# Conversion units among the experts on ScalarE's DMA queue, begun one unit ahead; x rows stored later; the last hidden tile halved first

## The chip, the cores and the metric

The kernel runs on one core of a Trainium2 chip. The metric is device time in microseconds of one execution. The engines are TensorE (PE), VectorE (DVE), ScalarE (ACT), GpSimd (POOL) and SyncE (SP); each works through its own instructions in order and waits for the others on semaphores. SyncE computes nothing and issues DMAs; ScalarE and GpSimd can issue DMAs too, from a queue of their own.

## The reference

Three stages follow one another.

- Attention for 4 batches and 12 heads, 448 positions, head size 64: `sigmoid(q k^T / 8 - log 448) v`. The heads are put side by side: x, 1792 rows of 768.
- A mixture of 8 experts: each row is routed to the expert with the largest cosine logit; `gate * (relu(x @ w1[e]) @ w2[e])`, with 1024 hidden columns.
- An FFN over all rows: `h = x @ w_in`, ELU, `@ w_out`, with 2048 hidden columns. `w_in` and `w_out` arrive as 64-bit floats.

## The kernel before

**Halves.** A float32 operand of a matmul is split into a high part (a ScalarE copy to a rounded type) and a low part (source minus high part, on VectorE), and each product is three matmuls: high by high, high by low, low by high. In `parts` these are lines 347 and 348; in `halves` lines 411 and 414.

**Attention.** Work goes by head pairs p = 0 to 23, six pairs to a batch. A pair has four quarters; in them TensorE does the scores of pair p (`S_part`, line 947), the products with v of pair p - 1 (`A_part`, line 966), and the transposes of q and k for pair p + 2 (`T_part`), which ScalarE and VectorE evacuate (lines 936, 938, 940). A list `late` holds jobs of the batch just finished, one taken in a quarter: logits, and `xrows`, which transposes x back to rows in a tile X (evacuated by VectorE, line 1051). `xstore` writes X to DRAM (line 1061). For the third batch the list also holds `early_a`, `early_b` and `early_c`; these find the rows of the first expert window from the first three batches and gather them (line 1139) for `x_first` (line 688), and from `early_b` on the first expert's weights are loaded.

**Conversion.** `conv_steps` turns the 64-bit words of `w_in` (layer 0, during the attention) and `w_out` (layer 1, among the experts) into float32 blocks, with sums of blocks for a seven-product (Strassen) FFN, and stores 28 blocks a layer to DRAM (`wdram`). It is a generator; `conv()` advances it by one step at places written out by hand. A layer has 16 units of 768 KB. A unit u has

- a load into tile c64 (tag c64, three buffers), issued by SyncE;
- a head: VectorE takes the upper word's magnitude bits into tile cm (line 146, which waits for the load), and GpSimd clamps it (line 150, "the clamp");
- step A (lines 200 to 220): VectorE puts sign, exponent and mantissa together (lines 209, 213), and the load of unit u + 2 is issued;
- step B (lines 221 to 237): VectorE adds the low word's share (lines 221, 224; the last reader of c64), and GpSimd adds the two parts into the result (line 234, "the add");
- step C (lines 238 to 242): the head of unit u + 2, then VectorE's sums for the unit before (line 169). Stores are issued four flushes after they are noted.

In the attention `conv()` stands in three of four quarters, from pair 2 on; among the experts it stands four times in a window.

**Experts.** Rows are sorted by expert into windows of 128; there are 19 in the regular loop here. Window w does the first layer of window w + 1 in four tiles (`L1_tile`, lines 707 to 709) with a conversion step after each, after the second of them the transposes of its own hidden rows (`hT_part`: line 728, hh on ScalarE at line 738, hl on VectorE at line 740), then the transposes of gathered rows for w + 2 (line 670, xh at 674, xl at 675), then its second layer in four tiles (`L2_tile`, line 769), and the gated evacuation y (line 751). The hidden rows come from ScalarE at line 713. Where a window has a new expert, weights are halved inside `tc.If`, and SyncE reloads the freed buffer with a conditional DMA:

```python
def parts_if(w, slots):
    with tc.If(new_of(w)):
        for slot in slots:
            parts(slot, nc.vector)
    for slot in slots:
        ...
        load_w(int(slot < 4), slot % 4, e, new=reg(nc.sync, "new", w))
```

`window(w)` calls it after its second and fourth second-layer tile, for w + 1 (second-layer weights) and w + 2 (first-layer weights). These loads are in the program whether or not the condition holds, each with its waits. At window 14 the conversion's memory is handed over to a tile r1, into which ScalarE's queue loads rows of y (line 423); from window 14 on rows of y are transposed and summed for the FFN.

**FFN.** `f1` (lines 1488 to 1490) and `f2` (lines 1620 to 1622) take 112 converted blocks, loaded by SyncE (line 385) and halved by `split_to`. B11, T2 and B21 are operands of x for it, the first units of which are halved around the last window.

Of the kernel before, what the change touches and what calls it, by code (L numbers as in the profile page):

```python
# [26 lines left out]
def kernel(  # L27
# [80 lines left out]
    w_out_b = w_out.bitcast(U32)  # L108
    NQ = F2 // 2 // 256

    def conv_steps(layer, cv, j0=0, j1=NQ):
        raw, mags, hf, sums, out = {}, {}, {}, [], []
        now = [0]

# [3 lines left out]
        def load(u):  # L118
            if u >= n:
                return  # L120
            j, qi = divmod(u, 4)
            r, c = quarters[qi]
            t = cv.tile([P, CU, 2], U32, tag="c64", bufs=3, name=f"c64_{layer}_{u}")
            raw[u] = t
            if layer == 0:
                c0 = 2 * (c * F2 // 2 + 256 * j)
                nc.sync.dma_start(
                    out=t.rearrange("p (k f) t -> p k (f t)", k=3),
                    in_=w_in_b[384 * r:384 * (r + 1), c0:c0 + 512].rearrange(
                        "(k p) f -> p k f", p=P  # L130
                    ),
                )
            else:
                r0 = r * F2 // 2 + 256 * j
                nc.sync.dma_start(
                    out=t.rearrange("p (k f) t -> p k (f t)", k=2),
                    in_=w_out_b[r0:r0 + 256, DM * c:DM * (c + 1)].rearrange(
                        "(k p) f -> p k f", p=P
                    ),
                )  # L140

        def head(u):
            if u >= n:
                return
            mags[u] = cv.tile([P, CU], U32, tag="cm", bufs=3, name=f"cm_{layer}_{u}")
            nc.vector.tensor_scalar(  # L146
                out=mags[u], in0=raw[u][:, :, 1], scalar1=0x7FFFFFFF, scalar2=None,
                op0=ALU.bitwise_and,
            )
            nc.gpsimd.tensor_scalar(  # L150
                out=mags[u].bitcast(F32), in0=mags[u].bitcast(F32), scalar1=F64_LEAST,
                scalar2=F64_MOST, op0=ALU.max, op1=ALU.min,
            )
# [5 lines left out]
        def flush(every=False):  # L159
            now[0] += 1  # L160
            while out and (every or out[0][0] <= now[0]):
                _, i, t = out.pop(0)
                nc.sync.dma_start(out=wdram[i], in_=t)

        def stile(name):
            return cv.tile([P, CU], F32, tag="cs", bufs=4, name=name)
# [28 lines left out]
            load(4 * j0 + u)  # L195
        yield
        head(4 * j0)
        head(4 * j0 + 1)
        yield
        for u in range(4 * j0, n):  # L200
            j, qi = divmod(u, 4)
# [16 lines left out]
            if u > 4 * j0:  # L218
                load(u + 2)
            yield  # L220
            nc.vector.tensor_scalar(
                out=mag, in0=cat, scalar1=0xFF800000, scalar2=None, op0=ALU.bitwise_and
            )
# [11 lines left out]
            sums.append((j, qi))  # L235
            flush()
            yield
            head(u + 2)
            if len(sums) > 1:
                group(*sums.pop(0))  # L240
            flush()
# [168 lines left out]
    def half_hi(src, hi):  # L410
        nc.scalar.activation(out=hi, in_=src, func=AF.Copy)  # L411
# [31 lines left out]
    def x_split(g, name):  # L443
        halves(xf[g][name], *xs2[g][name])
# [355 lines left out]
        for n in ("T1", "T2", "T3", "T4"):  # L800
            x_sum(0, n, slice(i * P, (i + 1) * P))

    def window(w, first, end, mid=None, turn=None):
        if w + 1 < end:
            more = w + 1
        else:
            more = None
        for t in range(4):
            if more:
                L1_tile(more, t)  # L810
            if t == 0:
                if w + 3 < end:
                    gather(w + 3)
                if w > max(first, 1):
                    scatter(w - 1)
            if t == 1:
                if w == 1:
                    route_step()
                hT_part(w, 1 if more else 2)
                if w == 1:  # L820
                    y_out(0)
                    scatter(0)
            conv(1)
        if w + 2 < end:
            xT_part(w + 2)
        if turn:
            turn()
        for t in range(4):
            L2_tile(w, t)
            if mid and t in mid:  # L830
                mid[t]()
            if t % 2 and first == 0:
                if w + 1 < end:
                    parts_if(w + 1, (3 + t, 4 + t))
                if w + 2 < end:
                    parts_if(w + 2, (t - 1, t))
# [28 lines left out]
    with ExitStack() as actx:  # L865
# [39 lines left out]
        nc.sync.dma_start(out=embt, in_=emb)  # L905
        nc.sync.dma_start(out=rtau, in_=tau.partition_broadcast(P))
        load(1, "qkv")
        conv_it[0] = conv_steps(0, cva)
        conv()

        pairs = [(b, hp) for b in range(B) for hp in range(NPAIR)]
# [236 lines left out]
        def after_pair(p):  # L1148
# [3 lines left out]
            if hp == NPAIR - 1:  # L1152
# [6 lines left out]
                late.append(lambda: xrows(b, 2, 1))  # L1159
                if b == B - 2:  # L1160
                    late.append(early_a)
                late.append(lambda: (xrows(b, 3, 1), xstore(b)))
                if b == B - 2:
                    late.append(early_b)
                if b == B - 2:
                    late.extend([lambda: None] * 2 + [early_c])
                squares.extend((b, c) for c in range(NCH))

        pw = ps_s.tile([P, 2, 512], F32, tag="s", name="pw")[:, 0, :]
# [104 lines left out]
    with mctx:  # L1274
# [50 lines left out]
        for w in range(1, NA):  # L1325
            if w == 4:
                n_win = nc.values_load(nwi, min_val=0, max_val=NW)
            if w == 2:
# [2 lines left out]
                cvb = yctx.enter_context(  # L1331
                    tc.tile_pool(name="cvb", bufs=1, side="right", reuse_waits="tile")
                )
                conv_it[0] = conv_steps(1, cvb)
                conv(2)
            if w == CE:
                def x_early(g):
# [27 lines left out]
                for u in range(4):  # L1365
                    load_u(u)
            else:
                window(w, 0, NA, turn=lambda: (x_split(0, "B11"), split_to(0)),
                       mid={1: lambda: (x_split(0, "T2"), split_to(1))})
                half_hi(xf[0]["B21"], xs2[0]["B21"][0])  # L1370
                split_to(2)
        scatter(NA - 1)
        with tc.If(n_win > NA):
            for w in range(NA, NW):
# [318 lines left out]
```

## Time and profile before

| | |
|---|---|
| runs | 1119.63 us median of 3 (1117.32 to 1122.5) |
| profiled execution | 1115.99 us, span 1114.1 us |
| TensorE busy | 1015.3 us (91% of the span) |
| VectorE busy | 747.9 us (67%) |
| ScalarE busy | 549.6 us (49%) |
| GpSimd busy | 269.0 us (24%) |
| mean granted TensorE clock | 0.966 of full speed |
| DMA | q1 (SyncE) 151.83 MB, q10 (ScalarE) 4.72 MB, q0 (GpSimd) 18.49 MB |

The attention takes about the first 230 us, the experts up to 655 us, the FFN the rest. Times in the views count from the start of the span. A row of a timeline gives start, duration, engine, line, operation and tiles, and in brackets how long the engine had been idle and what ended that. A row of the windows view gives a stretch, its length, the busy time and instruction count of PE, PEld (weight loads), DVE, ACT and POOL, the granted TensorE clock (1.00 is 2.4 GHz, the lower level 1.2 GHz is 0.5), and the DMA engines' busy share and rate in GB/s.

### The profile page before, as it was taken

The numbers are of one execution on the slowest core, as the hardware profiler recorded it, in microseconds if no ns is written. First come the engines' busy times: TensorE is split into PE (matmuls) and PEld (weight loads), VectorE is DVE, ScalarE is ACT, GpSimd is POOL, SyncE is SP. The second block draws the span as 40 slices with busy tenths as digits, with TensorE's granted clock in tenths as the row PEclk, the third lists the DMA queues.
The fourth block names the chain that finished last, engine by engine and source line by source line (L and its number), as shares of the span: only waits on it lengthen the run. The fifth ranks groups of instructions, "written<-read, shape, count | busy, mean of one in ns | idle before, by whom it ended". The sixth has DMA issues, their size and how long they took to land. (4 is left out here: it accounts for less than half of the span.)

```text
span 1114.1 us, 14875 instructions
## 1 busy us (share of the span) xinstructions
PE 1015.3 (91%) x5351; PEld 821.4 (74%) x5351; DVE 747.9 (67%) x853; ACT 549.6 (49%) x651; POOL 269.0 (24%) x189
## 2 busy tenths in 40 slices
PE   9997989988898797998989979999899999998997
PEld 5442434457797686987978967888898998997986
DVE  3898965376266484467335558888878578889883
ACT  6665566762224241234144556666643527677441
POOL 1665750054265253545201000000000040000002
PEclk9998999989999898999999989999899999999999
DMA  9678864544246676457266332332224353433342
GB/s 250 186 234 266 248 209 137 194 163 171 99 120 225 221 252 207 134 173 267 100 224 230 130 106 82 100 100 86 71 85 141 115 196 116 116 126 99 114 125 102
DMA packets 65520, 176.05 MB, mean 158 GB/s; under 512 B 6167, under 2 KB 22295, under 8 KB 64992
## 3 DMA queue, kind: packets, MB, share of 16 engines
q1 hardware_dynamic: 59840, 151.83, 43.1%
q0 software_dynamic: 4160, 18.49, 4.8%
q10 hardware_dynamic: 1440, 4.72, 1.2%
q8 instruction: 43, 0.70, 0.3%
q14 instruction: 37, 0.30, 0.1%
HBM read 211.98 MB, written 40.51 MB: 227 GB/s over the span
## 5 line engine op out<-in xcount | busy, mean ns | idle before, releaser
L150 POOL TENSOR_SCALAR cm<-cm 128x768 f32<-128x768 f32 x32 | 102.2, 3195 | 81.0 <-DVE cm L146 76.2
L708 PE MATMUL ph<-wl,xh 128*128 128x512 f32 x228 | 94.5, 415 | 20.9 <-DVEq L358 17.5
L769 PE MATMUL py<-wh,hh 128*128 128x384 f32 x304 | 106.1, 349 | 3.6 <-ACT hh L738 3.5
L348 DVE TENSOR_TENSOR wl<-raw,wh 128x1536 fp32r<-128x1536 f32 x44 | 76.3, 1775 | 43.5 <-ACT wh L347 42.9
L952 ACT ACTIVATE a<-ps,bias_s 112x896 f32<-112x896 f32 x96 | 91.6, 1002 | 26.2 <-PE ps L947 25.5
L769 PE MATMUL py<-wl,hh 128*128 128x384 f32 x304 | 103.6, 341 | 0.0
L707 PE MATMUL ph<-wh,xh 128*128 128x512 f32 x228 | 95.0, 417 | 7.1 <-ACT wh L347 5.5
L769 PE MATMUL py<-wh,hl 128*128 128x384 f32 x304 | 93.6, 339 | 0.1
L709 PE MATMUL ph<-wh,xl 128*128 128x512 f32 x228 | 93.0, 408 | 0.3 <-DVE xl L675 0.3
L947 PE MATMUL ps<-qk 64*112 64x448 f32 x384 | 87.7, 577 | 0.5 <-ACT a L952 0.5
L347 ACT ACTIVATE wh<-raw 128x1536 fp32r<-128x1536 f32 x48 | 69.2, 1481 | 31.5 <-DMA raw<-in_moe_w_dram 26.6
L414 DVE TENSOR_TENSOR wh<-raw,wh 128x768 fp32r<-128x768 f32 x65 | 61.8, 952 | 33.8 <-ACT wh L411 27.9
L966 PE MATMUL pav<-a,v 112*64 112x448 f32 x384 | 82.8, 553 | 0.0
L411 ACT ACTIVATE wh<-raw 128x768 fp32r<-128x768 f32 x65 | 54.4, 840 | 48.4 <-PE o L1622 31.4
L1621 PE MATMUL o<-wh,xr 128*128 128x384 f32 x196 | 68.7, 351 | 9.6 <-DVE wh L414 9.5
L708 PEld LDWEIGHTS ph<-wl,xh 128*128 128x128 f32 x228 | 45.4, 199 | 33.1 <-DVEq L358 19.3
L1620 PE MATMUL o<-wh,xr 128*128 128x384 f32 x196 | 67.3, 344 | 2.6 <-ACT wh L411 1.4
L1622 PE MATMUL o<-wh,xr 128*128 128x384 f32 x196 | 67.2, 343 | 2.3 <-DVE xr L414 2.3
L414 DVE TENSOR_TENSOR xr<-r,xr 128x1536 fp32r<-128x1536 f32 (+2 forms) x33 | 62.0, 1878 | 6.4 <-ACT xr L411 6.4
L740 DVE TENSOR_TENSOR hl<-pht,hh 128x1024 fp32r<-128x1024 f32 (+1 forms) x21 | 23.3, 1119 | 60.1 <-ACT hh L738 60.1
L966 PEld LDWEIGHTS pav<-a,v 112*64 112x64 f32 x384 | 23.5, 137 | 54.5 <-issue 51.6
L769 PEld LDWEIGHTS py<-wh,hh 128*128 128x128 f32 x304 | 58.5, 192 | 4.1 <-ACT hh L738 3.7
(291 smaller groups left out, 2500.9 us busy)
## 6 DMA issues: line engine op xcount, KB each, us to landing
raw<-in_moe_w_dram SPq DMA_DIRECT2D x142, 768.0 KB
raw<-wdram SPq DMA_DIRECT2D x112, 384.0 KB
c<-in_moe_w_in_dram SPq DMA_DIRECT2D x16, 768.0 KB
wdram<-ch SPq DMA_DIRECT2D x32, 384.0 KB
c<-in_moe_w_out_dram SPq DMA_DIRECT2D x16, 768.0 KB
wdram<-cs SPq DMA_DIRECT2D x24, 384.0 KB
v<-in_v_dram SPq DMA_DIRECT2D x12, 448.0 KB
xdram<-X SPq DMA_DIRECT2D x4, 1344.0 KB
```

Source lines behind the costliest of these rows:

```text
L150: nc.gpsimd.tensor_scalar(out=mags[u].bitcast(F32), in0=mags[u].bitcast(F32), scalar1=F64_LEAST, scalar2=F64_MOST, op0=ALU.max, op1=ALU.min,)
L347: nc.scalar.activation(out=wh, in_=raws[slot % 4], func=AF.Copy)
L348: eng.tensor_tensor(out=wl_, in0=raws[slot % 4], in1=wh.bitcast(F32), op=ALU.subtract)
L414: nc.vector.tensor_tensor(out=lo, in0=src, in1=hi.bitcast(F32), op=ALU.subtract)
L707: nc.tensor.matmul(o, lhsT=xh[:, kc, :], rhs=wh[:, sl], start=first, stop=False)
L708: nc.tensor.matmul(o, lhsT=xh[:, kc, :], rhs=wl_[:, sl], start=False, stop=False)
L709: nc.tensor.matmul(o, lhsT=xl[:, kc, :], rhs=wh[:, sl], start=False, stop=last)
L769: nc.tensor.matmul(py[:, n, :384], lhsT=a[:, f, :], rhs=b[:, i * 768 + n * 384:i * 768 + (n + 1) * 384], start=(f == 0 and a is hh and b i ...
L947: nc.tensor.matmul(ps[:CP, a, :S], lhsT=qk_t[p][r, 2, i * CP:(i + 1) * CP], rhs=qk_t[p][r, j, :], start=True, stop=True,)
L952: nc.scalar.activation(out=at, in_=ps[:CP, :, :S], func=AF.Sigmoid, bias=bias_s[:CP], scale=1.0 / math.sqrt(D),)
L966: nc.tensor.matmul(pav[p][j * D:(j + 1) * D, :S], lhsT=loaded[g][2][:, hh, c * D:(c + 1) * D], rhs=at_t[p, 2 * j + c // 2][:, c % 2, :], s ...
L1621: nc.tensor.matmul(o, lhsT=ah[:, c, ts_], rhs=wl_[:, sl], start=False, stop=False)
```

## The change

1. `conv_steps` takes the engine that issues its DMAs. Layer 0 stays on SyncE; all 16 loads and 28 stores of layer 1 go to ScalarE's queue.
2. The head of unit u + 1 is issued at the start of step B of unit u; before, the head of unit u + 2 was issued in step C of unit u. One unit's head, not two, is issued before the first step A. The tag cm has two buffers, not three.
3. `xstore` of the first two batches is taken from the list three jobs after the last `xrows` job; that of the third batch after `early_b`, two jobs after it. `early_c` keeps its place.
4. The last window's `hT_part` moves from that window into the one before it, behind its last second-layer tile and ahead of its `parts_if`. The halvings of B11 and unit 0 stand before the last window's first instruction, those of T2 and unit 1 after its first second-layer tile (before: after the second), those of B21 and unit 2 after its third (before: behind the window).

```diff
-    def conv_steps(layer, cv, j0=0, j1=NQ):
+    def conv_steps(layer, cv, eng, j0=0, j1=NQ):
...
-                nc.sync.dma_start(
+                eng.dma_start(
                     out=t.rearrange("p (k f) t -> p k (f t)", k=2),
...
-            mags[u] = cv.tile([P, CU], U32, tag="cm", bufs=3, name=f"cm_{layer}_{u}")
+            mags[u] = cv.tile([P, CU], U32, tag="cm", bufs=2, name=f"cm_{layer}_{u}")
...
                 _, i, t = out.pop(0)
-                nc.sync.dma_start(out=wdram[i], in_=t)
+                eng.dma_start(out=wdram[i], in_=t)
...
         head(4 * j0)
-        head(4 * j0 + 1)
         yield
...
             if u > 4 * j0:
                 load(u + 2)
             yield
+            head(u + 1)
             nc.vector.tensor_scalar(
                 out=mag, in0=cat, scalar1=0xFF800000, scalar2=None, op0=ALU.bitwise_and
             )
...
             flush()
             yield
-            head(u + 2)
             if len(sums) > 1:
                 group(*sums.pop(0))
...
-    def window(w, first, end, mid=None, turn=None):
+    def window(w, first, end, mid=None):
...
-                hT_part(w, 1 if more else 2)
+                if more:
+                    hT_part(w)
...
-        if turn:
-            turn()
         for t in range(4):
             L2_tile(w, t)
             if mid and t in mid:
                 mid[t]()
+            if t == 3 and w + 2 == end:
+                hT_part(w + 1, 2)
             if t % 2 and first == 0:
...
-        conv_it[0] = conv_steps(0, cva)
+        conv_it[0] = conv_steps(0, cva, nc.sync)
...
-                late.append(lambda: (xrows(b, 3, 1), xstore(b)))
+                late.append(lambda: xrows(b, 3, 1))
                 if b == B - 2:
                     late.append(early_b)
-                if b == B - 2:
-                    late.extend([lambda: None] * 2 + [early_c])
+                    late.extend([lambda: xstore(b), lambda: None, early_c])
+                else:
+                    late.extend([lambda: None] * 2 + [lambda: xstore(b)])
...
-                conv_it[0] = conv_steps(1, cvb)
+                conv_it[0] = conv_steps(1, cvb, nc.scalar)
...
-                window(w, 0, NA, turn=lambda: (x_split(0, "B11"), split_to(0)),
-                       mid={1: lambda: (x_split(0, "T2"), split_to(1))})
-                half_hi(xf[0]["B21"], xs2[0]["B21"][0])
-                split_to(2)
+                x_split(0, "B11")
+                split_to(0)
+                window(w, 0, NA, mid={
+                    0: lambda: (x_split(0, "T2"), split_to(1)),
+                    2: lambda: (half_hi(xf[0]["B21"], xs2[0]["B21"][0]), split_to(2)),
+                })
```

## Rows read from the trace of the kernel before

**Rows 1.** The waits, all engines: who waited for whom, us, times, longest
```profile
DVE cm L146 <- DMA c<-in_moe_w_out_dram: 41.8, 6, 13.3
...
DVE cm L146 <- DMA c<-in_moe_w_in_dram: 11.5, 2, 7.7
```

**Rows 2.** Windows: head pairs 4, 6, 10, 16; busy us, clock, DMA
```profile
39.20:47.93 8.73, 8.73 (x51) 4.00 (x49) 6.43 (x11) 5.43 (x7) 4.59 (x2) 1.00 0.66 191
56.03:63.79 7.76, 7.76 (x41) 3.03 (x40) 7.59 (x9) 5.43 (x8) 5.17 (x2) 1.00 0.86 243
90.30:108.50 18.20, 11.15 (x50) 4.78 (x49) 14.00 (x19) 7.34 (x12) 8.51 (x4) 0.81 0.98 287
151.50:167.33 15.83, 10.46 (x51) 4.69 (x49) 9.93 (x15) 7.35 (x12) 5.80 (x2) 0.89 0.74 231
```

**Rows 3.** Windows: expert windows 2, 5, 6, 8, 9, 12, 14, 15
```profile
292.80:317.92 25.12, 20.20 (x99) 18.36 (x99) 13.15 (x13) 3.83 (x5) 13.87 (x8) 0.86 0.48 159
354.13:380.52 26.39, 21.11 (x99) 18.33 (x98) 13.78 (x13) 6.46 (x7) 9.89 (x5) 0.87 0.60 197
380.52:408.28 27.76, 21.25 (x99) 18.46 (x99) 23.05 (x19) 12.31 (x11) 16.08 (x9) 0.82 0.75 252
427.48:453.66 26.18, 19.83 (x100) 17.55 (x100) 15.42 (x16) 3.72 (x5) 12.44 (x8) 0.87 0.56 185
453.66:471.76 18.10, 18.10 (x100) 16.55 (x100) 7.43 (x9) 3.73 (x5) 9.10 (x6) 1.00 0.41 134
510.68:534.96 24.28, 19.97 (x100) 17.63 (x100) 16.50 (x16) 6.46 (x7) 13.05 (x9) 0.93 0.59 200
553.06:579.36 26.30, 20.99 (x112) 19.08 (x112) 5.71 (x5) 8.34 (x11) 2.51 (x5) 0.94 0.48 169
579.36:599.70 20.34, 19.94 (x111) 17.75 (x111) 11.57 (x12) 11.08 (x13) 1.52 (x4) 1.00 0.68 227
```

**Rows 4.** Timeline of SyncE in window 5
```profile
358.15 16.11 SPq L338 DMA_DIRECT2D raw<-in_moe_w_dram  x8
...
374.32 0.40 SPq L135 DMA_DIRECT2D c<-in_moe_w_out_dram  x1
```

**Rows 5.** The waits of SyncE's own queue
```profile
SPq L1061 <- DVE X L1051: 38.9, 3, 21.8
```

**Rows 6.** Timeline of VectorE, pairs 4 and 5 and window 5
```profile
45.87 0.56 DVE L209 TENSOR_SCALAR cm<-cm 128x768 uint32<-128x768 uint32 x1
...
50.16 1.86 DVE L146 TENSOR_SCALAR cm<-c 128x768 uint32<-128x768 uint32 x1
...
379.91 0.56 DVE L146 TENSOR_SCALAR cm<-c 128x768 uint32<-128x768 uint32 x1 [8.55 <-DMA c<-in_moe_w_out_dram]
```

**Rows 7.** Timeline of GpSimd, the same pairs, and the first gather
```profile
44.34 2.77 POOL L150 TENSOR_SCALAR cm<-cm 128x768 f32<-128x768 f32 x1 [1.01 <-DVE cm L146]
...
49.79 1.81 POOL L234 TENSOR_TENSOR ch<-cm,cc 128x768 f32<-128x768 f32 x1 [2.67 <-DVE cm L224]
...
212.70 1.25 POOL L1139 DMA_INDIRECT xg<-xdram,idx  x1 [16.71 <-DMA xdram<-X]
```

**Rows 8.** Timeline of ScalarE at the start of window 14
```profile
563.37 1.81 ACTq L423 DMA_DIRECT2D r<-ydram  x4
...
565.28 1.02 ACT L738 ACTIVATE hh<-pht 128x1024 fp32r<-128x1024 f32 x1 [10.98 <-issue]
```

**Rows 9.** Timeline of TensorE: first gathered rows, last window, first FFN matmul
```profile
225.12 0.88 PE L688 MATMUL pxt<-ident,xg 128*128 128x128 f32 x6
...
644.57 0.45 PE L769 MATMUL py<-wh,hh 128*128 128x384 f32 x1 [3.48 <-ACT hh L738]
...
659.39 0.77 PE L1488 MATMUL f<-wl,wh 128*128 128x512 f32 x1 [4.37 <-DVEq L1373]
```

**Rows 10.** The page: a group of instructions, and a DMA's us to landing
```profile
L347 ACT ACTIVATE wh<-raw 128x1536 fp32r<-128x1536 f32 x48 | 69.2, 1481 | 31.5 <-DMA raw<-in_moe_w_dram 26.6
...
xg<-xdram,idx POOLq DMA_INDIRECT x1, 7.2
```

More of the change, by code (lines that the diff above doesn't have):

```diff
@@ L134, in load @@
                 r0 = r * F2 // 2 + 256 * j
-                nc.sync.dma_start(
+                eng.dma_start(
                     out=t.rearrange("p (k f) t -> p k (f t)", k=2),
```

## Prediction

> **What bounds the kernel now.** I began with the idle time of TensorE, because it is the engine that is busy nearly everywhere, and asked of each long gap what ended it. The waits give the first lead: VectorE waited 41.8 us in six places for the raw second-layer words (tile c, line 146, the head of a conversion unit) and 11.5 us in two places for the first-layer words [rows 1]. VectorE works in order, so whatever stands behind that head is late too: the evacuations of the attention's transposes, and in the experts the low halves of weights and the skipped `If` blocks that TensorE must see passed.
>
> Next I cut the span at stage borders. Head pairs 4, 10 and 16 do the same work in three batches (51, 50 and 51 recorded matmuls), but take 8.73, 18.20 and 15.83 us [rows 2]: the eight lost microseconds of each late pair are where the two waits of 11.5 us fall. An expert window without a wait takes 18.10 us (window 9), one with the extra rows of y 20.34 (window 15) [rows 3]. Against these, windows 2, 5, 6, 8, 12 and 14 are longer by 7.02, 8.29, 9.66, 8.08, 6.18 and 5.96 us. Not all of that is idle time. In window 8 TensorE idled 26.18 - 19.83 = 6.35 us, and its busy time is still 1.73 us above window 9's: after the idle stretch the granted clock averages 0.87, part of the window at the 1.2 GHz level and the rest at 2.4. So a long gap costs itself and some 1.7 us.
>
> Then SyncE, which issues all of these loads. In window 5 it spends 16.11 us on eight conditional weight loads, and only behind the last does the conversion's load leave, at 374.32; it lands at 379.9, where VectorE has idled 8.55 us [rows 4, 6]. The load was late in the queue, not long under way (5.6 us). In the attention the store of x rows holds the same queue for VectorE's last copy, 38.9 us in three waits [rows 5]. Last, two single gaps at the end of the experts: 3.48 us for hh of the last window, 4.37 us before the first FFN matmul [rows 9].
>
> **The change part by part.**
>
> *Experts: queue and order.* A load is issued at step A of the unit two before its own. Its head stood at step C of that same unit, two steps on; it moves to step B of the next, four steps on, which is one full window (18.10 us). Windows 5, 6, 8 and 12 wait because A and C fall into one window. On ScalarE's queue nothing conditional is ahead, so I expect all four waits to go. What comes instead: between a unit's head and its step A now lie the clamp (2.77 us) and, issued behind the clamp rather than before it, the add of the unit before (1.81 us) [rows 7]. That is 4.6 us on GpSimd, formerly spread over four steps. At best VectorE's own work covers it, at worst none; I take 2.3 us for windows 5, 6 and 12, where weights are halved right behind, and nothing for window 8, which has slack. Saved: 8.29 - 2.3 = 6.0, 9.66 - 2.3 = 7.4, 6.18 - 2.3 = 3.9 and 8.1 us, in all 25.4 (bounds 12.7, if contention with the weights keeps half, and 32.2).
>
> *Window 2.* Its first loads stay just ahead of their use, and they follow the evacuation of window 1 on ScalarE as they followed SyncE's last conditional load. I take 1.3 of 7.0 us (0 to 7.0).
>
> *Window 14.* ScalarE stands 10.98 us before hh, until four loads of y have been issued into memory that the last conversion stores must leave first [rows 8]. These stores now leave from ScalarE itself, not behind SyncE's eight loads; landing still takes its time. I take half, 3.0 us (0 to 5.96).
>
> *Cost on ScalarE.* 16 loads and 28 stores at 1.81/4 = 0.45 us each [rows 8] are 19.9 us of its queue in 12 windows, 1.7 each. In window 9 ScalarE is busy 3.73 of 18.10 us [rows 3], which hides them, unless one stands ahead of weight halves; 1.5 us in all (0 to 20). A load there waits for line 224 of a unit whose step B is two steps back; behind it on ScalarE stand the hidden layer's evacuations (lines 713 and 738), and TensorE waits for these.
>
> *Last window.* ScalarE copies hh before it halves two weight tiles of 1.48 us [rows 10]: 2.8 of the 3.48 us go. The halving of B21 and unit 2 moves ahead of the last evacuation, so before the FFN only that evacuation and the branch remain: 2.9 of 4.37 us (0 to 4.37). Both gaps then are too short to be followed by a slow stretch as in window 8, 1.7 us each. In all 9.1 us (3 to 11).
>
> *Attention.* The head moves two steps away from its load, and x rows are stored when VectorE is long done. VectorE's 11.5 us of waiting go. But VectorE is nearly full there, 7.59 of 7.76 us in pair 6 [rows 2], so any new hold costs TensorE time. Now the head comes right after the add and is held by it: 1.86 us at 50.16 against 0.56 for the same form at 45.87, during a clamp [rows 6, 7]. After, the add runs later and holds something else for up to 1.8 us. I take a net loss of 0.3 us in each of 16 units, 5 us, so 6.5 stay; and 2.5 of the 4.15 us that the two late pairs are busy beyond pair 4 twice (11.15 + 10.46 - 17.46). Together 9 us (3.5 to 16.6, the whole excess).
>
> *Third batch.* Its store goes two steps later, behind the first weight load on SyncE. The gather leaves at 212.70, lands 7.2 us later and is needed at 225.12: 5.2 us of cover [rows 7, 9, 10]. Two quarters of a pair of 8.73 us are 4.4 us: cost 0 (up to 4 if the weight load delays it further). The smaller ring of cm costs nothing while GpSimd's add is done one unit later.
>
> Sum: 25.4 + 1.3 + 3.0 - 1.5 + 9.1 + 9 = 46.3 us off the profiled execution's 1115.99, 1069.7. The median of the runs, 1119.63, is 3.6 above that execution: 1073 us.
>
> The VectorE row inside the clamp shows no hold and the one beside the add shows one. The Trainium skill (SBUF — State Buffer, "Who interferes with whom") says that VectorE in a two-port mode and GpSimd exclude each other for a whole instruction, whichever started first; by that, every clamp could hold the steps now right behind the head, and the first rival below would be the forecast. The row at 50.16 agrees with it for the add, the row at 45.87 does not for the clamp.
>
> **The rivals.**
>
> *GpSimd holds VectorE (slower).* If the clamp holds lines 221 and 224 in every unit, 16 units in a full VectorE lose the 2.77 us each, and 1.81 for the add: 73 us, against 37 saved elsewhere, 1073 + 9 + 73 = 1155; it decides from 37/16 = 2.3 us per unit. For it: VectorE's 98% in pair 6, and the 1.86 us. Against it: 0.56 us within the clamp, and two to three quarters of some 2.2 us between head and use. Chance 0.07.
>
> *The transfers, not the queue, were late.* Loads and stores then meet the weights in the engines: in pair 10 the DMA share was 0.98 and in window 6 0.75 [rows 2, 3]. The four windows keep half (12.7 more), the attention gains 3.5, window 14 nothing: 1073 + 12.7 + 5.5 + 3 = 1094. Against it: 5.6 us from issue to landing behind a wait of 16.11 [rows 4]. Chance 0.2. The Trainium skill (DMA: Bandwidth & Descriptors, "Issuing engines are not separate DMA queues") speaks for this rival: another engine's queue saves issue time only, as all run on the same 16 engines. The shares of 0.98 and 0.75 agree that the engines can be full; the 16.11 us ahead of the issue are no transfer.
>
> *ScalarE waits in its queue.* If a load or store stops it 3 us in each of 12 windows in front of an evacuation, 36 us go: 1109. For it: in-order issue; against it: its waits point two steps back. Chance 0.08.
>
> *Everything goes.* No new hold: the four windows give 32.2, window 14 5.96, the attention 16.6: 1054. Chance 0.1.
>
> **How the numbers follow.** The forecast has 0.55, with a range of its own of 1058 to 1088. From 1055 to 1100 it takes in the second rival and most of the last; left out are the first, most of the third and the lowest end, about 0.2. What a measurement can tell from no change is about 0.5%, 5.6 us, so same is 1114 to 1125. Faster: forecast, transfers, everything and most of the third, 0.87; same 0.05 from the third; slower 0.08, the first and an unseen cost.
>
> **What would show it.** Conversion loads on ScalarE's queue with no conditional load ahead; VectorE's line 146 without DMA waits but for the first of window 2; pairs 10 and 16 near 9 to 12 us; windows 5, 6, 8 and 12 near 18 to 21 us, window 2 still about 24; line 209 waiting for GpSimd at most 2 us; both single gaps under 1.5 us. I would be wrong if line 209's waits add up to tens of microseconds, if lines 713 and 738 come late behind DMA issues, or if the head still waits for c.

## The result and the profile after

The changed kernel takes 1077.15 us in the median of four runs (1073.87 to 1079.41); the kernel before, run beside it, 1119.29 (1117.32 to 1122.5). The ratio is 0.962, with a 95% interval of 0.959 to 0.965: 42 us faster. The forecast was 1073 us with 1055 to 1100, so time and sign came as predicted. Several terms of the sum did not; that their errors nearly cancel is luck.

The profiled execution of the changed kernel is the slowest of its four: 1079.41 us, span 1076.6, against 1115.99 and 1114.1 before. The stages below therefore show 37.5 us where the medians show 42.

Windows view of the changed kernel, expert windows 2, 5, 6, 7, 8, 12 and 14, cut at the same matmul as before [rows 3].

```profile
285.60:308.54 22.94, 19.71 (x99) 17.86 (x99) 10.59 (x12) 3.83 (x5) 12.21 (x7) 0.93 0.58 189
344.74:363.93 19.19, 18.51 (x99) 16.32 (x98) 13.46 (x12) 5.98 (x7) 9.98 (x6) 1.00 0.92 312
363.93:391.34 27.41, 21.20 (x99) 18.41 (x99) 20.48 (x17) 12.92 (x12) 11.67 (x5) 0.88 0.67 222
391.34:411.68 20.34, 18.36 (x99) 16.47 (x99) 15.83 (x15) 6.47 (x7) 11.35 (x8) 1.00 0.81 267
411.68:429.78 18.10, 18.10 (x99) 16.54 (x99) 9.85 (x11) 3.84 (x5) 8.05 (x5) 1.00 0.63 203
484.85:504.84 19.99, 18.37 (x99) 16.48 (x99) 16.82 (x15) 6.48 (x7) 11.91 (x7) 1.00 0.64 214
522.94:547.42 24.48, 21.22 (x111) 19.24 (x111) 5.70 (x5) 8.34 (x11) 2.51 (x5) 0.93 0.51 180
```

Windows 5, 8 and 12 lost 7.2, 8.1 and 4.3 us. Window 6 lost 0.35 (27.76 before), though 7.4 were forecast. Windows 2 and 14 lost 2.2 and 1.8. Window 7 grew by 1.1; window 11, not in the sum at all, lost 2.0 (20.82 to 18.87).

The same view, head pairs 10 and 16 [rows 2].

```profile
91.08:108.39 17.31, 11.53 (x51) 4.88 (x50) 16.88 (x23) 7.32 (x12) 9.89 (x5) 0.80 1.01 333
151.40:160.13 8.73, 8.73 (x51) 4.00 (x50) 8.53 (x11) 7.20 (x12) 6.08 (x3) 1.00 0.70 208
```

Pair 16 is as short as pair 4 was. Pair 10 hardly moved (18.20 to 17.31), and VectorE, busy 14.00 us there before, now is busy 16.88: it no longer waits for a transfer, it works.

The waits of the changed kernel (us, times, longest).

```profile
DVE cm L146 <- DMA c<-in_moe_w_out_dram: 12.2, 1, 12.2
...
DVE cm L208 <- POOL cm L150: 7.3, 6, 2.9
...
ACT xh L673 <- DMA raw<-in_moe_w_dram: 7.1, 1, 7.1
```

The waits of [rows 1], 41.8 and 11.5 us, are gone but for the first unit in window 2. The third row is odd: xh is a copy of transposed rows and reads no weights, yet it waits 7.1 us for a weight transfer. ScalarE's timeline there, in window 6, shows why.

```profile
355.50 1.09 ACT L712 ACTIVATE h<-ph 128x512 f32<-128x512 f32 x2 [3.51 <-PE ph L708]
363.23 0.39 ACTq L135 DMA_DIRECT2D c<-in_moe_w_out_dram  x1
363.72 0.81 ACT L673 ACTIVATE xh<-pxt 128x768 fp32r<-128x768 f32 x1 [7.13 <-DMA raw<-in_moe_w_dram]
367.60 2.86 ACT L346 ACTIVATE wh<-raw 128x1536 fp32r<-128x1536 f32 x2 [3.07 <-DMA raw<-in_moe_w_dram]
```

Ahead of xh stands the conversion's load (line 135). It could have left at 356.6, behind h, and left at 363.23. The records of the semaphore instructions say what the load waited for:

```
354.74  SyncE    DMA raw (weights), counts its landing on semaphore 106
363.17  SyncE    wait on 106 passes
363.17  ScalarE  wait on 106 passes (line 135)
363.23  ScalarE  DMA c (line 135), counts its landing on semaphore 106
```

In this trace the DMAs of SyncE and ScalarE take eight such semaphores, 101 and 103 to 109, in turn, in the order of the program, whichever of the two queues issues them. The load waited until the DMA eight places ahead, on its semaphore, had landed. That was a weight load of SyncE under way for 8.4 us.

TensorE stands still for 5.05 us from 364.1, and the granted clock averages 0.88 over the window. But the gap does not end with xh, which is done at 364.5; it ends with wh.

```profile
369.13 0.63 PE L706 MATMUL ph<-wh,xh 128*128 128x512 f32 x1 [5.05 <-ACT wh L346]
```

This halving waits for a conditional load that SyncE issues only at 367.46, because SyncE had stood until a second weight load, issued at 355.49, had landed (366.2, after 10.7 us). So late weights keep TensorE waiting, and xh's wait stands beside that.

Last, TensorE and VectorE at the start of the FFN.

```profile
610.16 0.44 PE L768 MATMUL py<-wh,hh 128*128 128x384 f32 x1 [0.74 <-ACT hh L737]
...
621.58 0.47 PE L1491 MATMUL f<-wl,wh 128*128 128x512 f32 x1 [2.80 <-DVEq L1376]
```

```profile
619.56 0.95 DVE L413 TENSOR_TENSOR wl<-raw,wl 128x768 fp32r<-128x768 f32 x1
620.43 0.95 DVE L413 TENSOR_TENSOR wh<-raw,wh 128x768 fp32r<-128x768 f32 x1
621.62 1.76 DVE L413 TENSOR_TENSOR xr<-r,wl 128x1536 fp32r<-128x1536 f32 x1 [0.24 <-DVEq L1376]
```

The gap for hh went from 3.48 to 0.74 us [rows 9]. The gap before the FFN went only from 4.37 to 2.80: the branch (line 1376) stands in VectorE's order behind the low halves of T2, unit 1 and unit 2, which moved ahead of it.

### The profile page after: what moved, and what is told of

It is laid out like the page before. It is cut to its first block, busy times and chain, and to the rows that moved or that the text cites. A ratio compares the mean times of both kernels' runs of the same rounds, so it can differ in the third digit from the quotient of the medians.

```text
span 1076.6 us, 14895 instructions
## 1 busy us (share of the span) xinstructions
PE 1006.1 (93%) x5351; PEld 814.9 (76%) x5351; DVE 758.7 (70%) x853; ACT 549.9 (51%) x651; POOL 265.4 (25%) x189
## 5 line engine op out<-in xcount | busy, mean ns | idle before, releaser
L150 POOL TENSOR_SCALAR cm<-cm 128x768 f32<-128x768 f32 x32 | 94.4, 2951 | 124.9 <-DVE cm L146 122.9
L706 PE MATMUL ph<-wh,xh 128*128 128x512 f32 x228 | 92.7, 407 | 6.6 <-ACT wh L346 5.0
L707 PE MATMUL ph<-wl,xh 128*128 128x512 f32 x228 | 91.9, 403 | 7.1 <-DVEq L357 5.1
L966 PEld LDWEIGHTS pav<-a,v 112*64 112x64 f32 x384 | 23.5, 137 | 54.6 <-issue 51.8
L1492 PE MATMUL f<-xr,wh 128*128 128x512 f32 (+1 forms) x162 | 59.0, 364 | 2.3 <-DVE xr L413 2.3
L739 DVE TENSOR_TENSOR hl<-pht,hh 128x1024 fp32r<-128x1024 f32 (+1 forms) x21 | 23.3, 1118 | 51.5 <-ACT hh L737 51.5
```

Of the source, the lines that this page charges most:

```text
L150: nc.gpsimd.tensor_scalar(out=mags[u].bitcast(F32), in0=mags[u].bitcast(F32), scalar1=F64_LEAST, scalar2=F64_MOST, op0=ALU.max, op1=ALU.min,)
L706: nc.tensor.matmul(o, lhsT=xh[:, kc, :], rhs=wh[:, sl], start=first, stop=False)
L707: nc.tensor.matmul(o, lhsT=xh[:, kc, :], rhs=wl_[:, sl], start=False, stop=False)
L966: nc.tensor.matmul(pav[p][j * D:(j + 1) * D, :S], lhsT=loaded[g][2][:, hh, c * D:(c + 1) * D], rhs=at_t[p, 2 * j + c // 2][:, c % 2, :], s ...
L1492: nc.tensor.matmul(o, lhsT=wh[:, sl], rhs=xl[:, kc, :], start=False, stop=False)
```

## The experiments

### Each part alone

Four kernels, each the kernel before with one part of the change. The kernel before, run beside them, took 1117.2 us.

Queue only (part 1):

```diff
...
-                conv_it[0] = conv_steps(1, cvb)
+                conv_it[0] = conv_steps(1, cvb, nc.scalar)
```

> The kernel before with one part of the change: the second layer's conversion loads and stores leave from ScalarE's queue; the head stays two steps behind its load. If the load was late because it stood behind SyncE's conditional loads (the prediction's reading), it now leaves at its step, lands some 6 us later and is there for the head in most windows: windows 5, 6, 8 and 12 lose at least half of their 32.2 us, 1119 - 16 to 25 = 1094 to 1103 us. If the distance between load and head is what counts, the four windows keep most of their excess: 1110 to 1119 us. The attention (pairs 10 and 16 at 18.2 and 15.8 us) and the end of the experts stay as they were.

1097.74 us, ratio 0.982 (0.977 to 0.986). Waits of its VectorE:

```profile
DVE cm L146 <- DMA c<-in_moe_w_out_dram: 21.3, 6, 12.1
...
DVE cm L146 <- DMA c<-in_moe_w_in_dram: 12.2, 2, 7.7
```

41.8 us of waiting became 21.3: window 8 fell to 18.10 us, windows 5, 6 and 12 only to 23.59, 25.34 and 20.61. So the queue was a cause, as predicted, but with two steps between load and head its change is no full cure.

Head only (part 2):

```diff
...
-        head(4 * j0 + 1)
...
+            head(u + 1)
             nc.vector.tensor_scalar(
...
-            head(u + 2)
```

> The kernel before with one part alone: the head of unit u + 1 in step B of unit u, one head ahead instead of two, two buffers of cm; loads and stores of both layers stay on SyncE. If the distance of four steps (18.1 us) covers a load that leaves 16 us late, windows 5, 6, 8 and 12 fall by 20 to 25 us and the attention's late pairs by 5 to 9: 1085 to 1094 us. If the queue has to be free for it, the windows keep over half of their excess and the time stays above 1103 us.

1090.92 us, ratio 0.977 (0.973 to 0.980). Its windows 2, 5, 6 and 8:

```profile
286.07:310.82 24.75, 20.45 (x100) 18.60 (x100) 11.13 (x13) 3.83 (x5) 12.21 (x7) 0.86 0.52 175
347.02:366.20 19.18, 18.48 (x99) 16.47 (x99) 14.52 (x13) 6.47 (x7) 10.19 (x6) 1.00 0.68 214
366.20:391.06 24.86, 21.21 (x100) 18.26 (x100) 19.35 (x16) 12.31 (x11) 11.50 (x5) 0.86 0.87 321
411.40:429.50 18.10, 18.10 (x100) 16.54 (x100) 9.74 (x11) 3.72 (x5) 8.06 (x5) 1.00 0.71 237
```

Windows 5 and 8, and 12 with 20.00 us, are those of the full change to 0.01 us, with every load still behind SyncE's conditional loads. Window 6 is no longer than there either. A head one window behind its load covers the queue; the other queue adds nothing there.

Store of x rows only (part 3):

```diff
-                late.append(lambda: (xrows(b, 3, 1), xstore(b)))
+                late.append(lambda: xrows(b, 3, 1))
...
+                    late.extend([lambda: None] * 2 + [lambda: xstore(b)])
```

> The kernel before with one part alone: the store of x rows is taken from the list later. If the store, waiting in SyncE's queue for VectorE's last copy, is what made the first layer's words late, VectorE's 11.5 us of waits for them go, pair 16 falls from 15.8 to about 9 us and pair 10 from 18.2 to 11 to 17: 1119 - 7 to 12 = 1107 to 1112 us. If the short distance between load and head was the cause, both pairs stay: 1116 to 1121 us.

1106.08 us, ratio 0.990 (0.987 to 0.993). Its pairs 10 and 16:

```profile
90.40:104.33 13.93, 10.59 (x50) 4.33 (x49) 13.60 (x18) 7.31 (x12) 8.50 (x4) 0.88 1.06 342
147.56:156.29 8.73, 8.73 (x50) 3.99 (x49) 8.44 (x13) 7.21 (x12) 5.68 (x2) 1.00 0.63 208
```

The waits for the first layer's words are gone altogether, and the first score matmul of the last pair starts at 207.4 us, against 218.4 before, 212.1 with the head alone and 211.2 with the full change. In the attention the store does all of it, and the new order of the heads takes some of it back: 3.8 us by these starts, of which 0.7 arise before pair 2 (it starts at 24.0 us in the changed kernel, at 23.3 here). From pair 2 to the last pair the changed kernel takes 187.2 us, this one 184.0.

Last window only (part 4):

```diff
...
+            if t == 3 and w + 2 == end:
+                hT_part(w + 1, 2)
...
```

> The kernel before with one part alone: the last window's hidden tile halved one window earlier, the FFN's first operands halved earlier in the last window. By the stages of the changed kernel 4.6 us in the last window and 1.6 before the FFN, 6.2 in all: 1113 us, if this part does not lean on the others. By the prediction's sum 9.1 us: 1110 us. If the last window was late for another reason (the conversion's end), under 3 us.

1111.04 us, ratio 0.994 (0.992 to 0.996): 6.8 us. Its two gaps are 0.74 and 2.83 us, as in the full change, so this part leans on no other.

The four parts alone give 20.3 + 26.3 + 11.2 + 6.8 = 65 us (one minus the ratio, times 1117.2), the whole 42. Queue and head cure the same windows, store and head the same pairs.

### Why window 6 stayed long

Stores of the second layer on GpSimd's queue, in the changed kernel:

```diff
-                eng.dma_start(out=wdram[i], in_=t)
+                (eng, nc.gpsimd)[layer].dma_start(out=wdram[i], in_=t)
```

> The changed kernel, but the second layer's 28 stores leave from GpSimd's queue; its loads stay on ScalarE. Theory of the shared counters: ScalarE stands 7.1 us before xh of window 6 because its conversion load, the fourth DMA after eight weight loads of SyncE, is to count its landing on the semaphore that the fourth of those weight loads still counts on; without three stores ahead it takes the semaphore of the first, which landed long before, so the stall goes, window 6 falls from 27.4 to about 20 us and the time by some 7 us, to 1070 us. Rival: the DMA engines are full (0.9 and more busy there), the load is late anyway: window 6 stays at 26 to 28 us and the time at 1077 us. A third outcome: GpSimd's own cost of issuing stores delays clamp and add, and windows 2 to 14 grow.

1071.14 us, ratio to the kernel before 0.958 (0.956 to 0.960); this interval just meets that of the change, so it is the stages that tell. Windows 6, 7 and 14:

```profile
363.47:385.65 22.18, 19.07 (x100) 16.38 (x99) 19.20 (x16) 11.02 (x11) 12.51 (x7) 1.00 0.77 266
385.65:407.75 22.10, 19.97 (x99) 17.61 (x99) 16.16 (x15) 6.46 (x7) 12.92 (x10) 0.92 0.67 237
519.01:538.87 19.86, 19.69 (x112) 17.77 (x111) 5.55 (x5) 8.35 (x11) 3.79 (x7) 1.00 0.57 190
```

The load takes semaphore 109 and leaves at 355.84, right behind h; xh waits 0.33 us, and the clock stays at 1.00. Window 6 loses 5.2 us, window 7 gives 1.8 back, and window 14 loses 4.6. There the last of the stores leaves at 518.70, and ScalarE's loads of y, which go into memory that the stores read, 4.1 us later:

```profile
518.70 0.54 POOL L163 DMA_DIRECT2D wdram<-cs  x1 [1.58 <-DVE cs L169]
```

```profile
522.76 2.00 ACTq L422 DMA_DIRECT2D r<-ydram  x4
```

In the changed kernel the last store leaves at 526.95, 4.0 us into window 14, and the loads from 531.05.

The same stores on SyncE's queue:

```diff
-                eng.dma_start(out=wdram[i], in_=t)
+                nc.sync.dma_start(out=wdram[i], in_=t)
```

> The changed kernel, but the second layer's stores leave from SyncE again; its loads stay on ScalarE. Theory of the shared counters: which queue issues does not matter, the order of issue in the program gives the semaphore, so the load of window 6 still takes that of the fourth weight load and ScalarE still stands there: window 6 stays at 26 to 28 us, 1077 us or a few more if SyncE's stores are late for the window 14 handover. Rival: ScalarE's own three stores just ahead of the load in its queue hold it up: window 6 falls to about 20 us, 1070 us.

1075.03 us, ratio 0.961 (0.960 to 0.963). Window 6 and ScalarE in it:

```profile
360.82:383.36 22.54, 19.16 (x100) 16.39 (x99) 19.20 (x16) 11.42 (x11) 11.34 (x5) 1.00 0.79 263
```

```profile
355.05 0.81 ACT L673 ACTIVATE xh<-pxt 128x768 fp32r<-128x768 f32 x1 [1.71 <-PE py L768]
```

What the theory of shared semaphores forecast for window 6 missed. The load does take 106 again, behind the weight load that left at 350.30, and its wait passes at 354.52, some 1.2 us behind h: that weight load landed after 4.2 us, where its 768 KB took 8.4 in the changed kernel. There three stores of 384 KB left from ScalarE beside it (354.05 to 354.97); here they follow at 356.82. Window 7 takes 22.13 us, window 14 still 25.64, for on SyncE the last store leaves at 522.36, 5.5 us into that window, and the loads of y again 4.2 us later. The semaphore decides who waits; how long goes with the stores beside the weights.

Stores two flushes later, still from ScalarE:

```diff
-            out.append((now[0] + 4, i, t))
+            out.append((now[0] + (4, 6)[layer], i, t))
```

> The changed kernel, but the second layer's stores are issued six flushes after they are noted, not four, from ScalarE's queue as before; so in window 6 the load stands ahead of its three stores and is the first DMA after the eight weight loads, not the fourth. Theory of the shared counters: it takes the semaphore of the first weight load, which has landed, so the wait ahead of xh goes from 7.1 us to under 1, and the wait moves to the stores; window 6 falls from 27.4 to 20 to 23 us, 1072 us. Rival, that only full DMA engines delay ScalarE's load: the same traffic in the same stretch, window 6 stays above 26 us, 1077 us.

1077.28 us, ratio 0.963 (0.961 to 0.966): no gain. ScalarE and window 6:

```profile
355.89 0.37 ACTq L135 DMA_DIRECT2D c<-in_moe_w_out_dram  x1
356.36 0.81 ACT L673 ACTIVATE xh<-pxt 128x768 fp32r<-128x768 f32 x1 [0.33 <-ACT h L712]
364.16 2.86 ACT L346 ACTIVATE wh<-raw 128x1536 fp32r<-128x1536 f32 x2 [6.98 <-DMA raw<-in_moe_w_dram]
```

```profile
363.52:388.06 24.54, 21.41 (x99) 18.55 (x99) 19.68 (x16) 12.43 (x11) 11.82 (x5) 0.86 0.71 261
```

One store (352.78) still stands ahead of the load, which is thus the second DMA behind the eight weight loads, not the first as expected; it takes semaphore 103, and its wait is gone as the theory says (7.13 to 0.33 us). But wh still comes at 364.16: SyncE stands until the weight load that left at 354.12 has landed, after 8.6 us. Window 6 loses 2.9 us, windows 2, 12 and 14 give 2.2 back. Two kernels of the next part (the first layer in the old order, and no steps in two passes), with the changed kernel's code in the experts, have window 6 at 24.94 and 25.29 us with the same wait ahead of xh (5.4 us); so 2 to 2.5 of the 27.41 us are of that one execution, and this kernel gains 0.4 to 0.8, GpSimd's queue 2.8 to 3.1. ScalarE's wait is real, but taken away alone it is worth next to nothing, because the weights are late.

How late they are goes with the stores issued just ahead of them or between them, and the window goes with it. Time from issue to landing of the two weight loads, by the counts of their semaphores, and window 6 (the kernels differ in more than this, so it is a relation and no price):

| kernel | stores beside them | first, us | second, us | window 6, us |
|---|---|---|---|---|
| changed kernel | 3 | 8.4 | 10.7 | 27.41 |
| no steps; first layer old | 3 | 7.3, 6.9 | 9.4, 9.0 | 25.29, 24.94 |
| stores two flushes later | 1 | 7.0 | 8.6 | 24.54 |
| stores on GpSimd | 0 | 4.3 | 5.6 | 22.18 |
| stores on SyncE | 0 | 4.2 | 5.5 | 22.54 |
| the faster one; its loads on SyncE | 0 | 4.4, 4.2 | 5.6, 5.4 | 21.77, 21.67 |

### Why pair 10 stayed long

Head behind the add in step B:

```diff
-            head(u + 1)
             nc.vector.tensor_scalar(
...
             nc.gpsimd.tensor_tensor(out=o, in0=v[0], in1=v[1], op=ALU.add)
+            head(u + 1)
```

> The changed kernel, but the head of the next unit is issued behind the add of step B instead of ahead of its step. Theory that the add holds one VectorE instruction wherever it stands (up to 1.9 us): only another instruction is held, pairs 10 and 16 stay at 17.3 and 8.7 us within 2 us, 1077 us. Rival: that the clamp stands ahead of the add, so that the add meets the long sums of step C and the copies of q and k, is the cost in the attention: pair 10 falls by 3 us or more, 1073 us. In the experts the clamp ends 1.8 us later, which has cover of two steps.

1090.23 us, ratio 0.975 (0.973 to 0.977): 13 us slower than the changed kernel, outside both expectations. Pair 10 did fall, to 15.96, but pairs 7, 8, 14 and 16 grew, and the last pair begins at 219.1, 7.9 us later. Among the experts windows 11 and 12 grew too, by 1.9 and 3.5 us: the cover expected there did not hold. The costliest groups by line from 20 to 205 us, on VectorE (busy us, mean ns, idle before), in three kernels. The changed kernel:

```profile
L224 DVE SCALAR_TENSOR_TENSOR cm<-c,cm 128x768 f32<-128x768 uint32 x16 | 22.3, 1396 | 0.6
...
L208 DVE TENSOR_SCALAR cm<-cm 128x768 uint32<-128x768 uint32 x16 | 16.1, 1007 | 2.4 <-POOL cm L150 2.2
...
L146 DVE TENSOR_SCALAR cm<-c 128x768 uint32<-128x768 uint32 x16 | 8.9, 554 | 0.1
```

The kernel before with the later store alone, in the old order of heads:

```profile
L224 DVE SCALAR_TENSOR_TENSOR cm<-c,cm 128x768 f32<-128x768 uint32 x16 | 15.3, 958 | 0.6
L146 DVE TENSOR_SCALAR cm<-c 128x768 uint32<-128x768 uint32 x16 | 14.3, 901 | 0.1
...
L209 DVE TENSOR_SCALAR cm<-cm 128x768 uint32<-128x768 uint32 x16 | 13.5, 842 | 0.9 <-POOL cm L150 0.7
```

This kernel:

```profile
L208 DVE TENSOR_SCALAR cm<-cm 128x768 uint32<-128x768 uint32 x16 | 8.9, 558 | 20.0 <-POOL cm L150 19.9
```

In the new order line 224 runs beside the clamp in 14 of 16 units and takes 1.46 us in each of them; in the other two, and in all 16 of the old order (one of them with 0.6 us of the clamp beside it), it takes 0.96. That is 1396 ns instead of 958 in the mean, 7.0 us over 16 units; line 208 (209 with the store alone), beside the add, costs 2.6 more, the sums of line 169 cost 3.3 more (21.1 against 17.8). Line 146 is freed of 5.4 us, lines 938, 212 and 221 of 3.4. That is 4.1 us more for VectorE, and from pair 2 on TensorE lost 3.2 (184.0 to 187.2). With the add in front the holds on both lines go (958 and 558 ns), but the clamp ends too late and VectorE waits 19.9 us for it. I read both as one shortage, which no run varied alone: one head ahead leaves clamp and add one unit's time, two heads ahead left two.

First layer in the old order, the rest as changed:

```diff
...
+            if layer == 1:
+                head(u + 1)
...
+            if layer == 0:
+                head(u + 2)
```

> The changed kernel, but the first layer's units keep the old order (head of unit u + 2 in step C, three buffers of cm); the second layer and the stores of x rows stay as changed. Theory: with the x rows stored later the new order gains nothing in the attention and costs what GpSimd then holds of VectorE; the kernel before with the later store alone had pair 10 at 13.9 us and reached the last pair at 207.4 us, the changed kernel 17.3 and 211.2. So pair 10 falls to about 14 us and the time by 3.8 us, to 1073 us. Rival: the 3.8 us came from the start of the run or from chance: no change.

1071.87 us, ratio 0.958 (0.956 to 0.961). Pair 10 takes 13.89 us, and the last pair begins at 207.5: as expected, though 1.3 of the 3.7 us are the start of the run (pair 2 begins at 22.7). From pair 2 to the last it is 184.8 us; four kernels with the new order (the changed one and the three with moved stores) take 187.0 to 187.3. So the new order costs 2.2 to 3.3 us in the attention, not 3.8.

No conversion steps in loop passes 9 and 10:

```diff
-                if 2 <= p < NP_ - 1 and (i != 1 or p % 4 == 0):
+                if 2 <= p < NP_ - 1 and (i != 1 or p % 4 == 0) and p not in (9, 10):
```

> The changed kernel, but no conversion step is taken in loop passes 9 and 10 of the attention; the two units come later, in passes 18 to 20, where VectorE has 1.9 to 6 us of work in 8. Theory: pair 10 takes 17.3 us because VectorE falls behind (97 of 100 busy from pair 5 to 17, and x rows of the batch on top in pairs 7 to 10): the 5.8 us gap there goes, pair 10 falls to about 9 to 11 us, and the time by 6 to 8 us, to 1070 us. Rival: the gap comes with the x rows and the waits for GpSimd whatever the conversion does, or the backlog only moves to a later pair: no change, 1077 us.

1073.58 us, ratio 0.961 (0.958 to 0.964). Its pairs 10 and 16:

```profile
90.03:100.48 10.45, 8.95 (x51) 3.98 (x50) 4.98 (x13) 7.21 (x12) 0.31 (x1) 1.00 1.02 306
144.62:154.35 9.73, 8.94 (x51) 3.97 (x50) 9.47 (x13) 7.21 (x12) 6.24 (x3) 1.00 0.97 277
```

Without the steps the gap is gone: 6.9 us less in pair 10, 1.0 more in pair 16, the last pair at 205.5, 5.7 us earlier. So it came with the conversion's work on VectorE there, GpSimd's holds included, which go with it, and not with the x rows alone. The medians do not show the 6 to 8 us expected: the interval overlaps that of the change.

### What is faster than both

The changed kernel with the first layer in the old order, no steps in passes 9 and 10, the second layer's stores on GpSimd's queue, and at the end of the experts (held_t2 halves T2 and unit 1 and keeps their low halves back):

```diff
...
+                window(w, 0, NA, mid={0: held_t2})
+                held = lows[:]
+                lows.clear()
...
+        for f in held:
+            f()
+        half_hi(xf[0]["B21"], xs2[0]["B21"][0])
+        split_to(2)
```

> The changed kernel with four edits that act on different stretches: the first layer in the old order, no conversion step in loop passes 9 and 10, the second layer's stores on GpSimd's queue, and in the last window the low halves of T2 and unit 1 behind the branch and B21 and unit 2 behind the window. If the stages add up: attention 3.8 + 5 us, windows 6, 7 and 14 together 7.9 us, the gap before the FFN from 2.8 to 1.5 us: 1077 - 18 = 1059 us. If VectorE's hold and the backlog in pair 10 are one and the same gain, 1063 us. Rival for the gap before the FFN: it is set by ScalarE's last evacuation, and stays at 2.8 us.

1060.22 us, ratio to the kernel before 0.948 (0.945 to 0.951), below the interval of the change. Pairs 10 and 16, windows 6 and 14, and the 21.2 us from the end of the experts:

```profile
90.11:98.83 8.72, 8.72 (x50) 3.99 (x49) 4.07 (x10) 7.21 (x12) 0.86 (x1) 1.00 0.95 294
142.73:153.28 10.55, 8.96 (x51) 3.97 (x50) 10.29 (x14) 7.22 (x12) 6.58 (x2) 1.00 1.01 290
...
356.68:378.45 21.77, 18.89 (x100) 16.40 (x99) 19.01 (x16) 10.58 (x10) 12.53 (x7) 1.00 0.77 262
510.19:530.04 19.85, 19.68 (x111) 17.77 (x111) 5.55 (x5) 8.33 (x11) 3.79 (x7) 1.00 0.58 192
```

```profile
601.29:622.50 21.21, 20.04 (x89) 16.61 (x89) 14.38 (x12) 15.30 (x15) 1.02 (x1) 1.00 0.37 114
```

The stages nearly add up: the last pair begins at 204.3, 6.9 us earlier where 8.8 were expected, and the gap before the FFN is 1.17 us. After it the clock stays at 1.00 and 89 matmuls are recorded; in the changed kernel, after 2.80 us, 0.92 and 74 in as long. Little of it lasts: the FFN then takes 455.65 us from its first matmul, against 455.03.

The same with the second layer's loads on SyncE:

```diff
-                conv_it[0] = conv_steps(1, cvb, nc.scalar)
+                conv_it[0] = conv_steps(1, cvb, nc.sync)
```

> The version of the four edits (1060 us), with the second layer's 16 loads back on SyncE, behind its conditional weight loads, and its stores on GpSimd as there. Theory: once the head stands a window behind its load, the queue that issues the load gives nothing; windows 5, 8, 9 and 12 stay at 19.2, 18.1, 18.1 and 20.0 us, and only window 2, whose first loads have no such distance, grows by 1 to 2 us: 1058 to 1063 us. The prediction's reading, that a load must not stand behind the conditional loads: the waits of the head for tile c come back in windows 5 to 12, 10 us or more: above 1069 us.

1063.43 us, ratio 0.950 (0.949 to 0.952). Windows 2, 5 and 6:

```profile
279.78:304.84 25.06, 20.74 (x99) 18.88 (x99) 11.41 (x13) 3.83 (x5) 12.21 (x7) 0.86 0.50 173
341.04:360.21 19.17, 18.47 (x99) 16.47 (x99) 14.78 (x14) 8.24 (x9) 10.88 (x9) 1.00 0.75 251
360.21:381.88 21.67, 18.81 (x99) 16.37 (x99) 18.96 (x16) 10.55 (x10) 12.50 (x7) 1.00 0.84 335
```

Only window 2 differs by more than 0.3 us, 25.06 against 22.73; window 8 takes 18.10 in both. Head alone, with its loads on SyncE too, had 24.75 there, the kernels with early head and loads on ScalarE 21.4 to 23.5. The intervals of the two kernels overlap, so it is the stage that tells: with the head early, the loads' queue is worth some 2 us, in window 2.

## Why the prediction was right, and where it was not

**The four windows, 25.4 us forecast, 19.9 measured.** The mechanism was right in windows 5, 8 and 12 (the load behind the conditional loads, too short a way from load to head), and the size too: 6.0, 8.1, 3.9 against 7.2, 8.1, 4.3. The reason was half right. "On ScalarE's queue nothing conditional is ahead" named the queue as the cure; head alone and the loads back on SyncE show that the distance is enough. Window 6 is the term that failed, 7.4 against 0.35 (2.5 to 2.8 in the two kernels with the same code): VectorE's wait went, and late weights took its place. Moving the DMAs put three stores beside the weights, which then landed after 6.9 to 10.7 us, against 4.5 and 5.7 in the kernel before. It also brought ScalarE behind SyncE's weight loads by their shared semaphores, which the prediction had not seen; that alone cost next to nothing. This is the second rival's contention in one place, with the third rival's wait beside it.

**The transfers.** The Trainium skill (DMA: Bandwidth & Descriptors, "Issuing engines are not separate DMA queues") says that another issuing engine saves issue time only. With heads one window ahead the runs agree but for some 2 us in window 2; with the old order it was worth 20 us, since the time ahead of the issue was a wait of the queue and no transfer.

**Windows 2 and 14.** 1.3 and 3.0 forecast, 2.2 and 1.8 measured. Window 2's first loads did better than their term, 1.3 of 7.0. For window 14 the mechanism held, only the landing takes longer than the half allowed: in the kernels compared the loads of y leave some 4 us behind the last store. It gave 4.6 more once the stores left earlier, on GpSimd's queue.

**Last window and FFN start, 9.1 forecast, some 6 measured.** hh came as worked out: 2.7 us of the gap, and from there to the end of the window the clock averages 1.00, as forecast. The gap before the FFN failed: of "only that evacuation and the branch remain" the runs showed the low halves moved ahead of the branch as well. With them behind it the gap is 1.17. Nor was this gap "too short to be followed by a slow stretch": the clock averages 0.92 behind it in this execution.

**Attention, 9 forecast, 7.2 measured.** The parts inside were the right ones: 11 us from the transfers' waits, less what GpSimd holds. The hold was put at 5 us net; the groups by line give 4.1, and 2.2 to 3.3 reached TensorE. What failed is the other side of the term: "VectorE's 11.5 us of waiting go" was put to the head's distance and the store together, and the store alone has all of it, so the new order is a loss in the attention. The first rival, that the clamp holds line 224, is there with 0.44 us a unit in the mean, under the 2.3 from which it decides.

**The sum.** 46.3 forecast for the profiled execution, 37.5 measured by its span, 42 in the medians. Window 11's 2.0 us, unforeseen, stood against the misses, and the profiled execution was the slowest of its four. That the median lies 4 us from the forecast is in part luck.

## What to carry to other kernels

Before moving a transfer to another queue, ask whether an earlier issue or a later use covers the wait: the two cures do not add, and the queue brings its own waits with it. Look at what is in flight beside the transfers that other engines wait for: here stores beside the weights cost about 3 us of one window. Where DMAs of two engines take their completion semaphores in one rotation, as in these traces, a DMA can wait for the landing of the other engine's, and everything behind it on its engine does too. Price each part in its own stage and run each alone; a part that costs (here the new order in the attention) hides behind one that cures the same wait.

## What the hardware showed unexpectedly

- The first 768 KB weight load ahead of window 6 landed 6.9 to 8.4 us after its issue in three kernels with three stores of 384 KB issued from ScalarE beside it, after 7.0 with one, and after 4.2 to 4.5 in six with none.
- Inside GpSimd's clamp line 224, with two inputs from SBUF, took 1.46 us instead of 0.96, in 14 units of 16: 0.5 us more, beside a clamp of 2.9 us. Line 221, with one input, stayed at 553 ns in the mean (572 before), but ran beside the clamp for some 0.3 us only. The Trainium skill (SBUF — State Buffer, "Who interferes with whom") names this case too: two SBUF inputs contend with a GpSimd instruction that reads SBUF. The runs agree; the prediction had weighed only the two-port half of that page.
- After the gap of 2.80 us before the FFN the granted clock averaged 0.92 over the next 21.2 us, after one of 1.17 us it was 1.00. The length of the gap alone does not tell: after 2.83 us it was 0.86 with the stores on SyncE and 1.00 in the kernel with part 4 alone.
